# Window attention and two gated MLPs: where the second MLP's weights are decoded

## The chip, the cores and the metric

One NeuronCore of a Trainium2 chip runs the whole program in one launch. The metric is the device time of an execution in microseconds; lower is better. Inputs lie in the chip's DRAM as 64-bit floats, the output is 32-bit. The engines are TensorE (PE, with its weight load PEld), VectorE (DVE), ScalarE (ACT), GpSimd (POOL) and SyncE (SP, which issues the DMAs).

## The reference

Attention over a window of 64 keys (4 x 8 heads, 576 positions, head width 64) gives x of 2304 tokens by 512. Two gated MLPs follow, each with two matrices of 512 by 1536 and one of 1536 by 512:

```python
x = (1 / (1 + np.exp(-(x @ w_gate))) * (x @ w_val)) @ w_out
x = ((x @ w_a) * (x @ w_b)) @ w_out
```

## The kernel before

**Weights.** They come as 64-bit floats, two 32-bit words an element. A weight is *decoded* in bulk: `decode_words` (L369) makes the bits of a 32-bit float from the two words (ScalarE: `low` L374 and `ex` L377; VectorE: `wi` L380, L383 and, for the second MLP, the addition L387), and `decode_pair` (L391) multiplies (L393, VectorE) and splits the weight in a high and a low part (L399 ScalarE, L402 VectorE, GpSimd for `o`), which are multiplied as three products so that the sum is exact enough. F counts the slices of 128 hidden columns: 0 to 11 are the first MLP, 12 to 23 the second (NF = 12). Each F has three matrices, `a`, `b` and `o`. The parts are stored (`save`), to be fetched again for the tokens that come later.

**Tokens.** They are cut into blocks of 256: block 0 alone, 1 to 4 in pairs ("front"), 5 to 8 ("back", a second pass over all weights). For the front's blocks 1 to 4 the second MLP multiplies 2 by 2 blocks with seven products in place of eight. One such set for one F is a *quad* (L912): products 1, 5, 6, 2, 7, 4, 3 in this order, of six matmuls each into three PSUM banks (`qa`, `qb`, `qc`), with sums kept aside in `r` tiles (L865, pool `rs`), sums added (L868), the gate (L878) and the split of the hidden values (L470, L472). Products 5, 6, 7, 3 need sums and differences of the halves of `a` and `b`: `combining` (L416) makes these four *combinations*, each by a GpSimd addition (`s`, L439), a ScalarE copy (`wq`, L441) and a GpSimd subtraction (L442), and stores them.

**Order.** Up to the tenth turn of the first MLP the order on every engine is written out. After that the program gives instructions out in an order of its own, and a scheduler with a timeline simulation makes each engine's queue from it at build: an instruction may go ahead of earlier ones on its engine if the simulation has it ready sooner. An engine runs its queue in order. A manual dependency of class NoSync keeps the scheduler from putting an instruction ahead of another; it makes no wait on the chip.

`step_decode` (L659) does one step of decoding: it finishes one matrix, or one half of a combination. F may be decoded when the buffers of F - 4 are past their last use and F is within `limit`. For the second MLP's quads, `begin_matrix` (L641) starts the words of the next matrix one step ahead of its pair; those of F = NF + 2 are held behind the instruction that stands ahead of the first quad (L1132). The loop at L1139 goes over the twelve quads. In its gaps (`between`, L1160) it takes work off a list (`fill`: the output banks of the two quads before, L984) and takes a decoding step after every product but the fourth. In quad fc, F = NF + fc + 2 is decoded. Ahead of quads 0, 2 and 4, block 0's own hidden values for two F are made (L1141 to L1148: `hidden`, matmuls L461, `hr` L485). The pools of this stretch are opened at L1074. Ahead of the first quad come the last sums of the first MLP (`gacc`, L539; `xh`, `xl`, L570, L571) and the operands of the seven products (L749, L755, L758).

Of the kernel before, what the change touches and what calls it, by code (L numbers as in the profile page):

```python
# [21 lines left out]
def tile_window_attention_gated_mlps(ctx, tc, q, k, v, w1g, w1v, w1o, w2a, w2b, w2o, out):  # L22
# [346 lines left out]
    def decode_words(F, i, nm):  # L369
        st = staged.pop((F, nm))  # L370
        w0, w1 = st[:, :, 0], st[:, :, 1]
        k = 3 * F + i if F > NF + 2 else 0
        low = dec.tile([P, DM], I32, tag="low", name="low")
        nc.scalar.activation(out=low, in_=w0.bitcast(U32), func=AF.Copy, scale=2.0 ** -29)  # L374
        yield
        ex = late["dec"].tile([P, DM], F32, tag="ex", name="ex") if k % 3 == 2 else dec.tile([P, DM], F32, tag="ex", bufs=2, name="ex")
        nc.scalar.activation(out=ex, in_=w1.bitcast(F32), func=AF.Abs)  # L377
        yield
        wi = (late["dec"] if k % 2 else dec).tile([P, DM], I32, tag="wi", name="wi")
        nc.vector.tensor_scalar(  # L380
            out=wi, in0=w1, scalar1=3, scalar2=(1 << 30) - 1, op0=ALU.logical_shift_left, op1=ALU.bitwise_and
        )
        nc.vector.scalar_tensor_tensor(  # L383
            out=wi, in0=w1, scalar=-(1 << 30), in1=wi, op0=ALU.bitwise_and, op1=ALU.bitwise_or
        )
        yield
        (nc.vector if F >= NF else nc.gpsimd).tensor_tensor(out=wi, in0=wi, in1=low, op=ALU.add)  # L387
        wordy[F, nm] = ex, wi
        yield
# [24 lines left out]
    pairs, full = {}, {}  # L414

    def combining(F):  # L416
        got = combinations(parts[F], full.pop((F, "a")), full.pop((F, "b")))
        for half in range(2):
            for n, t in islice(got, 2):
                nc.sync.dma_start(out=kept_q[F - NF][:, n], in_=t.bitcast(F32))  # L420
            yield

    kept_q = [dram.tile([P, 4, 2, CH], F32, tag=f"kq{p}", name=f"kq{p}") for p in range(NF)]

    def halves(got):
        got[1], got[2] = (tuple(p[:, j * CH:(j + 1) * CH] for p in got["a"]) for j in range(2))
        if "b" in got:
            got[4] = tuple(p[:, CH:] for p in got["b"])
# [3 lines left out]
    def combinations(got, a, b):  # L432

        halves(got)
        (a1, a2), (b1, b2) = ((f[:, 0:CH], f[:, CH:]) for f in (a, b))

        def combined(n, nm, x, y, op):
            s = late["sts"].tile([P, CH], F32, tag="s", name=f"s{nm}")
            nc.gpsimd.tensor_tensor(out=s, in0=x, in1=y, op=op)  # L439
            t = late["wq"].tile([P, 2, CH], F32R, tag="wq", name=f"wq{nm}")  # L440
            nc.scalar.activation(out=t[:, 0], in_=s, func=AF.Copy)  # L441
            nc.gpsimd.tensor_tensor(out=t[:, 1], in0=s, in1=t[:, 0].bitcast(F32), op=ALU.subtract)  # L442
            got[nm] = (t[:, 0], t[:, 1])
            return s, (n, t)

        s1, t = combined(0, 5, b1, b2, ALU.add)
        yield t
        s2, t = combined(1, 6, s1, a1, ALU.subtract)
        yield t
        yield combined(2, 7, a1, b1, ALU.subtract)[1]  # L450
        yield combined(3, 3, a2, s2, ALU.subtract)[1]
# [183 lines left out]

    limit = [NF - 1]
    order = [(F, i, nm) for F in range(DECODED, NW) for i, nm in enumerate("abo")]
    held = [None]
    begun, pending, combined_by = [0], [], []

    def begin_matrix():  # L641
        if begun[0] == 0:
            load_weights(DECODED)
        if begun[0] < len(order):
            F, i, nm = m = order[begun[0]]
            begun[0] += 1
            since = len(nc.cur_bb.bb.instructions)
            whole(decode_words(*m))
            if F == NF + 2 and held[0]:
                for i in nc.cur_bb.bb.instructions[since:]:  # L650
                    tc.add_manual_dep(
                        i, held[0],
                        mybir.DependencyInfo(mybir.DependencyClass.NoSync, mybir.DependencyReason.DATA), reason="held",
                    )
            pending.append(m)
            if F + 1 < NW:
                load_matrix(F + 1, nm)

    def step_decode(turn):  # L659

        if combined_by:
            if next(combined_by[0], combined_by) is not combined_by:
                return True
            combined_by.pop()
        if not pending:
            begin_matrix()
        if not pending:
            return False
        F, i, nm = m = pending[0]
        if F > limit[0] or (F > G and last_use.get(F - G - 1, -1) >= turn):  # L670
            return False
        if F >= NF + 2:
            begin_matrix()
        pending.pop(0)
        whole(decode_pair(*m))
        save(F, nm, pairs.pop((F, nm)))
        if nm == "o":
            ready[F] = parts[F]
        elif nm == "b" and F >= NF:
            combined_by.append(combining(F))  # L680
        return True
# [382 lines left out]
    for n, (group, fcs) in enumerate(plan):  # L1064
        begin, end = fcs[0] == 0, fcs[-1] == NF - 1
        if n < len(FIRST):
            continue
        if n == SPAN.start:
            attend(FRONT[-1][-1])
            feed = attention_stream(BACK[BEHIND:])  # L1070
        if n == SPAN.stop:
            attend(BACK[-1])
            attend(steps=100)
            next_part(early, (("op6", 1), ("hs", 1), ("wq", 8), ("sts", 3), ("rs", 2), ("dec", 1)), middle)  # L1074
            limit[0] = NF + 1
        hs = []
        for i, fc in enumerate(fcs):
            need(fc, n)
            hs.append((ready[fc], hidden(0, ready[fc], x[0, group])))
            for _ in range(-(-len(queue) // (len(fcs) - i))):  # L1080
                queue.pop(0)()
            for _ in group:
                for _ in range(2 if late else 1):
                    step_decode(n)
                if late and not combined_by:
                    step_sums()
                if n in SPAN:
                    due += STEPS / ticks
                    attend(steps=int(due))
                    due -= int(due)  # L1090
        queue.append(lambda a=(group_of[group[0]], group, hs, begin, end): [(m(), e()) for m, e in first_projection(*a)])
        if n == len(plan) - 2:
            built = front_operands(FRONT[2], FRONT[1])
            x_ops = next(built)
# [34 lines left out]
    ALONE = {0: (0, 1), 2: (2, 3), 4: (4, 5)}  # L1129
    BETWEEN, LATER = (9, 10, 11), (6, 7, 8)  # L1130
    nquad[0] = 1
    held[0] = next(reversed(nc.cur_bb.bb.instructions)).name  # L1132
    hs, h0s, res = [], [], None
    seconds = (
        lambda: late["hs"].tile([P, 2, W], F32R, tag="hs", name="h1"),
# [3 lines left out]
    for fc in range(NF):  # L1139
# [19 lines left out]

        def between(i):  # L1160
            fill(counts[0][i] + (extra if i == 4 else 0))
            if i != 3:
                step_decode(NEVER)

        hs.append((w["o"], quad(1, w, x_ops, between, g, seconds[fc % 3], lambda: None)))
        if len(hs) == PAIR:
# [161 lines left out]
```

## Time and profile before

| | us |
|---|---|
| median of 3 runs | 962.4 |
| lowest and highest | 962.11, 963.88 |
| the profiled execution | 961.65 |
| its span, first to last instruction | 959.8 |
| granted TensorE clock, mean | 0.996 |

The profile is of one execution. Busy times are of the span or of a stretch of it, in microseconds from its start. A wait is the time in which an engine stood before an instruction, put down to what released it. The rows say `line engine op out<-in`; `st_a` is a staged matrix of words, `wq` a combination, `accm` a bank of the first MLP's output and `accq` one of the second's.

### The profile page before, as it was taken

How to read it: one execution, taken by the hardware profiler on the slowest of the kernel's cores; microseconds unless marked ns; L12 is line 12 of the kernel's file. 1: busy time of each engine (PE TensorE's matmuls, PEld its weight loads, DVE VectorE, ACT ScalarE, POOL GpSimd, SP SyncE). 2: the span in 40 equal slices, each digit the busy share in tenths (PEclk: the TensorE clock that was granted, in tenths of full speed). 3: DMA queues.
4: the chain of work that ended last, by engine and by line, in shares of the span. 5: the costliest groups of instructions: out<-in, count | busy, mean ns of one | idle time of the engine just before them, and what ended most of it. 6: DMA issues, size and time to landing. Idle time of an engine off the chain costs nothing.

```text
span 959.8 us, 15660 instructions
## 1 busy us (share of the span) xinstructions
PE 926.2 (96%) x5504; PEld 774.3 (81%) x5504; DVE 708.0 (74%) x1379; ACT 480.2 (50%) x1063; POOL 311.8 (32%) x321
## 2 busy tenths in 40 slices
PE   7899999999999888899999998999999999999998
PEld 6798888887887777788787886788888888888886
DVE  6997887886568898969989566778888673354545
ACT  7897555687645456654545334654454243211111
POOL 4543222342236727434545127644440000000000
PEclk9999999999999999999999999999999999999999
DMA  8987598988468537755665447354446674554322
GB/s 216 246 240 223 206 327 284 330 287 248 143 229 307 211 142 249 245 202 182 241 217 200 176 155 262 110 176 164 142 155 209 219 263 149 168 167 131 98 66 87
DMA packets 144685, 193.69 MB, mean 202 GB/s; under 512 B 63584, under 2 KB 98912, under 8 KB 143968
## 3 DMA queue, kind: packets, MB, share of 16 engines
q1 hardware_dynamic: 144608, 192.71, 61.9%
q8 instruction: 43, 0.70, 0.3%
q14 instruction: 34, 0.28, 0.1%
HBM read 118.75 MB, written 69.47 MB: 196 GB/s over the span
## 4 chain that ended last, share of the span: by engine, by line
PE 70%; DVE 13%; issue 4%; POOL 4%; DMA 4%; ACT 4%; SPq 0%; DVEq 0%; POOLq 0%; ACTq 0%
PE qa L846 16%; PE accq L984 11%; PE qb L846 8%; PE gps L461 7%; PE vps L461 7%; PE accm L562 6%; PE qc L846 4%; PE accy L947 3%; PE accx L947 2%; POOL s L439 2%; DVE wi L387 2%; DVE wi L383 2%; DVE ex L393 2%; PE xps L228 2%; PE sps L170 1%
## 5 line engine op out<-in xcount | busy, mean ns | idle before, releaser
L865 ACT ACTIVATE r<-qa 128x512 f32<-128x512 f32 x108 | 63.4, 595 | 105.3 <-PE qa L846 95.5
L442 POOL TENSOR_TENSOR wq<-s,wq 128x256 fp32r<-128x256 f32 x96 | 85.4, 895 | 93.0 <-ACT wq L441 88.2
L846 PE MATMUL qa<-op,wq 128*128 128x512 f32 x432 | 112.5, 390 | 0.7 <-ACT op L749 0.6
L846 PE MATMUL qb<-op,wq 128*128 128x512 f32 x432 | 110.5, 390 | 1.5 <-DVE qc L868 1.2
L461 PE MATMUL gps<-xh,wa 128*128 128x256 f32 (+1 forms) x392 | 104.9, 338 | 4.4 <-ACT xh L570 2.3
L461 PE MATMUL vps<-xh,wb 128*128 128x256 f32 (+1 forms) x392 | 105.7, 339 | 3.3 <-ACT hr L485 3.3
L846 PEld LDWEIGHTS qb<-op,wq 128*128 128x128 f32 x432 | 80.9, 188 | 19.0 <-DVE qc L868 1.7
L846 PEld LDWEIGHTS qa<-op,wq 128*128 128x128 f32 x432 | 80.8, 188 | 17.9 <-ACT op L749 0.8
L562 PE MATMUL accm<-hh,wo 128*128 128x512 f32 (+1 forms) x296 | 84.6, 355 | 2.6 <-DVE gacc L539 2.6
L387 POOL TENSOR_TENSOR wi<-wi,low 128x512 int32<-128x512 int32 x36 | 50.0, 1388 | 112.2 <-DVE wi L383 71.3
L461 PEld LDWEIGHTS gps<-xh,wa 128*128 128x128 f32 x392 | 68.7, 189 | 13.8 <-ACT xh L570 2.6
L461 PEld LDWEIGHTS vps<-xh,wb 128*128 128x128 f32 x392 | 69.4, 191 | 11.2 <-ACT hr L485 3.6
L984 PE MATMUL accq<-wo,h 128*128 128x512 f32 (+1 forms) x300 | 71.1, 382 | 1.7 <-DVE resf L988 1.6
L461 PE MATMUL gps<-xl,wa 128*128 128x256 f32 (+1 forms) x196 | 65.8, 336 | 1.0 <-DVE xl L237 0.6
L393 DVE SCALAR_TENSOR_TENSOR ex<-ex,wi 128x512 f32<-128x512 f32 x72 | 52.3, 727 | 18.7 <-ACT ex L377 13.4
L461 PE MATMUL vps<-xl,wb 128*128 128x256 f32 (+1 forms) x196 | 65.9, 336 | 0.0
L984 PEld LDWEIGHTS accq<-wo,h 128*128 128x128 f32 x300 | 55.0, 188 | 13.4 <-DVE resf L988 2.3
L470 ACT ACTIVATE hh<-qa 128x512 fp32r<-128x512 f32 x36 | 21.5, 597 | 84.6 <-DVE qa L878 55.6
L562 PEld LDWEIGHTS accm<-hh,wo 128*128 128x128 f32 x296 | 53.0, 189 | 11.7 <-DVE gacc L539 3.7
L984 PE MATMUL accq<-wo,hh 128*128 128x512 f32 x184 | 55.7, 393 | 3.4 <-ACT hh L470 2.2
L189 ACT ACTIVATE pr<-pr,stat 128x128 f32<-128x128 f32 x144 | 54.0, 390 | 7.5 <-DVE stat L183 7.3
L846 PE MATMUL qa<-op,wa 128*128 128x512 f32 x216 | 57.0, 395 | 0.4 <-DVE g L868 0.4
(178 smaller groups left out, 2137.4 us busy)
## 6 DMA issues: line engine op xcount, KB each, us to landing
wo<-ko SPq DMA_DIRECT2D x27, 512.0 KB, 4.2
wa<-ka SPq DMA_DIRECT2D x27, 512.0 KB, 4.4
st_o<-in_moe_w_out_dram SPq DMA_DIRECT2D x24, 512.0 KB, 4.9
ka<-wa SPq DMA_DIRECT2D x24, 512.0 KB, 4.7
kb<-wb SPq DMA_DIRECT2D x24, 512.0 KB, 3.9
ko<-wo SPq DMA_DIRECT2D x24, 512.0 KB, 4.1
kq<-wq SPq DMA_DIRECT2D x48, 256.0 KB, 3.5
wq<-kq SPq DMA_DIRECT2D x48, 256.0 KB, 3.2
```

The costliest lines, as they stand in the source:

```text
L189: nc.scalar.activation(out=pr[e][:, j, :], in_=pr[e][:, j, :], func=AF.Exp, bias=nmax[:, e, j:j + 1], scale=-1.0, accum_out=None if t in O ...
L228: nc.tensor.matmul(xps[dims, j, rows], lhsT=vv[:, 2 * j + e, :], rhs=pt[e][:, j, rows], start=True, stop=True)
L387: (nc.vector if F >= NF else nc.gpsimd).tensor_tensor(out=wi, in0=wi, in1=low, op=ALU.add)
L393: nc.vector.scalar_tensor_tensor(out=wf, in0=wf, scalar=SMALLEST, in1=wi.bitcast(F32), op0=ALU.is_ge, op1=ALU.mult)
L442: nc.gpsimd.tensor_tensor(out=t[:, 1], in0=s, in1=t[:, 0].bitcast(F32), op=ALU.subtract)
L461: nc.tensor.matmul(ps, lhsT=a[:, c * P:(c + 1) * P], rhs=b[:, c, :], start=(n == 0), stop=(n == 3 * NP - 1))
L470: nc.scalar.activation(out=hh, in_=hr, func=AF.Copy, scale=factor)
L562: nc.tensor.matmul(ps[:, m], lhsT=a[:, sl], rhs=b, start=k == 0, stop=k == total - 1)
L846: nc.tensor.matmul(ps, lhsT=a[:, c * P:(c + 1) * P], rhs=b[:, c, :], start=first and n == 0, stop=n == 5, skip_group_check=True,)
L865: nc.scalar.activation(out=r[n], in_=ps, func=AF.Copy)
L947: nc.tensor.matmul(bank[k], lhsT=a[n][i][:, sl], rhs=b[n][j], start=start and m == 0, stop=m == 2, skip_group_check=True,)
L984: nc.tensor.matmul(ps, lhsT=a, rhs=b, start=n == 0, stop=n == len(pairs) - 1)
```

## The change

The tiles `ex` and `wi` lose their extra buffers, and `begin_matrix` is now called by the step that also finishes the matrix, so no words are made a step ahead; the hold at the first quad goes. A combination is made in three steps: all four sums on GpSimd, then all four copies on ScalarE, then the four subtractions on GpSimd and the stores; the second of them goes together with the next matrix in one call. In the quads the steps are taken by `paced`, which ties the step's instructions, but those of SP, to the last matmul given out ahead of it. Quad 0 takes its six steps two each after products 7, 4 and 3; the others one after every product but the fourth, as before. The pools: `sts` 4 for 3, `rs` 3 for 2, the second `dec` pool gone.

```diff
@@ -369,14 +369,13 @@
     def decode_words(F, i, nm):
         st = staged.pop((F, nm))
         w0, w1 = st[:, :, 0], st[:, :, 1]
-        k = 3 * F + i if F > NF + 2 else 0
         low = dec.tile([P, DM], I32, tag="low", name="low")
         nc.scalar.activation(out=low, in_=w0.bitcast(U32), func=AF.Copy, scale=2.0 ** -29)
         yield
-        ex = late["dec"].tile([P, DM], F32, tag="ex", name="ex") if k % 3 == 2 else dec.tile([P, DM], F32, tag="ex", bufs=2, name="ex")
+        ex = dec.tile([P, DM], F32, tag="ex", bufs=2, name="ex")
         nc.scalar.activation(out=ex, in_=w1.bitcast(F32), func=AF.Abs)
         yield
-        wi = (late["dec"] if k % 2 else dec).tile([P, DM], I32, tag="wi", name="wi")
+        wi = dec.tile([P, DM], I32, tag="wi", name="wi")
         nc.vector.tensor_scalar(
             out=wi, in0=w1, scalar1=3, scalar2=(1 << 30) - 1, op0=ALU.logical_shift_left, op1=ALU.bitwise_and
         )
@@ -414,11 +413,23 @@
     pairs, full = {}, {}
 
     def combining(F):
-        got = combinations(parts[F], full.pop((F, "a")), full.pop((F, "b")))
-        for half in range(2):
-            for n, t in islice(got, 2):
-                nc.sync.dma_start(out=kept_q[F - NF][:, n], in_=t.bitcast(F32))
-            yield
+        got = parts[F]
+        halves(got)
+        (a1, a2), (b1, b2) = ((f[:, 0:CH], f[:, CH:]) for f in (full.pop((F, nm)) for nm in "ab"))
+        sums = {}
+        for nm, x, y, op in ((5, b1, b2, ALU.add), (6, 5, a1, ALU.subtract), (7, a1, b1, ALU.subtract), (3, a2, 6, ALU.subtract)):
+            sums[nm] = s = late["sts"].tile([P, CH], F32, tag="s", name=f"s{nm}")
+            nc.gpsimd.tensor_tensor(out=s, in0=sums[x] if isinstance(x, int) else x, in1=sums[y] if isinstance(y, int) else y, op=op)
+        yield
+        tiles = {}
+        for nm, s in sums.items():
+            tiles[nm] = t = late["wq"].tile([P, 2, CH], F32R, tag="wq", name=f"wq{nm}")
+            nc.scalar.activation(out=t[:, 0], in_=s, func=AF.Copy)
+        yield
+        for n, (nm, t) in enumerate(tiles.items()):
+            nc.gpsimd.tensor_tensor(out=t[:, 1], in0=sums[nm], in1=t[:, 0].bitcast(F32), op=ALU.subtract)
+            got[nm] = (t[:, 0], t[:, 1])
+            nc.sync.dma_start(out=kept_q[F - NF][:, n], in_=t.bitcast(F32))
 
     kept_q = [dram.tile([P, 4, 2, CH], F32, tag=f"kq{p}", name=f"kq{p}") for p in range(NF)]
 
@@ -635,8 +646,8 @@
 
     limit = [NF - 1]
     order = [(F, i, nm) for F in range(DECODED, NW) for i, nm in enumerate("abo")]
-    held = [None]
-    begun, pending, combined_by = [0], [], []
+    parts_done = [0]
+    begun, combined_by = [0], []
 
     def begin_matrix():
         if begun[0] == 0:
@@ -644,34 +655,26 @@
         if begun[0] < len(order):
             F, i, nm = m = order[begun[0]]
             begun[0] += 1
-            since = len(nc.cur_bb.bb.instructions)
             whole(decode_words(*m))
-            if F == NF + 2 and held[0]:
-                for i in nc.cur_bb.bb.instructions[since:]:
-                    tc.add_manual_dep(
-                        i, held[0],
-                        mybir.DependencyInfo(mybir.DependencyClass.NoSync, mybir.DependencyReason.DATA), reason="held",
-                    )
-            pending.append(m)
             if F + 1 < NW:
                 load_matrix(F + 1, nm)
 
     def step_decode(turn):
 
         if combined_by:
-            if next(combined_by[0], combined_by) is not combined_by:
+            parts_done[0] += 1
+            if next(combined_by[0], combined_by) is combined_by:
+                combined_by.pop()
+                parts_done[0] = 0
                 return True
-            combined_by.pop()
-        if not pending:
-            begin_matrix()
-        if not pending:
+            if parts_done[0] == 1:
+                return True
+        if begun[0] == len(order):
             return False
-        F, i, nm = m = pending[0]
+        F, i, nm = m = order[begun[0]]
         if F > limit[0] or (F > G and last_use.get(F - G - 1, -1) >= turn):
             return False
-        if F >= NF + 2:
-            begin_matrix()
-        pending.pop(0)
+        begin_matrix()
         whole(decode_pair(*m))
         save(F, nm, pairs.pop((F, nm)))
         if nm == "o":
@@ -1071,7 +1074,7 @@
         if n == SPAN.stop:
             attend(BACK[-1])
             attend(steps=100)
-            next_part(early, (("op6", 1), ("hs", 1), ("wq", 8), ("sts", 3), ("rs", 2), ("dec", 1)), middle)
+            next_part(early, (("op6", 1), ("hs", 1), ("wq", 8), ("sts", 4), ("rs", 3)), middle)
             limit[0] = NF + 1
         hs = []
         for i, fc in enumerate(fcs):
@@ -1129,7 +1132,19 @@
     ALONE = {0: (0, 1), 2: (2, 3), 4: (4, 5)}
     BETWEEN, LATER = (9, 10, 11), (6, 7, 8)
     nquad[0] = 1
-    held[0] = next(reversed(nc.cur_bb.bb.instructions)).name
+
+    def paced():
+
+        made = nc.cur_bb.bb.instructions
+        since = len(made)
+        at = next(i.name for i in reversed(made) if i.engine == mybir.EngineType.PE)
+        step_decode(NEVER)
+        for i in nc.cur_bb.bb.instructions[since:]:
+            if i.engine != mybir.EngineType.SP:
+                tc.add_manual_dep(
+                    i, at, mybir.DependencyInfo(mybir.DependencyClass.NoSync, mybir.DependencyReason.DATA), reason="paced"
+                )
+
     hs, h0s, res = [], [], None
     seconds = (
         lambda: late["hs"].tile([P, 2, W], F32R, tag="hs", name="h1"),
@@ -1159,8 +1174,8 @@
 
         def between(i):
             fill(counts[0][i] + (extra if i == 4 else 0))
-            if i != 3:
-                step_decode(NEVER)
+            for _ in range(((0, 0, 0, 0, 2, 2, 2) if fc == 0 else (1, 1, 1, 0, 1, 1, 1))[i]):
+                paced()
 
         hs.append((w["o"], quad(1, w, x_ops, between, g, seconds[fc % 3], lambda: None)))
         if len(hs) == PAIR:
```

## Rows read from the trace of the kernel before

**Rows 1.** The page, part 1: busy us, share of the span, instructions.
```profile
PE 926.2 (96%) x5504; PEld 774.3 (81%) x5504; DVE 708.0 (74%) x1379; ACT 480.2 (50%) x1063; POOL 311.8 (32%) x321
```

**Rows 2.** Busy time by stretch; PEclk is the granted clock's mean share.
```profile
core 0: us, PE busy (x) PEld busy (x) DVE busy (x) ACT busy (x) POOL busy (x), PEclk, DMA share, GB/s
...
300.00:336.00 36.00, 32.42 (x150) 26.12 (x149) 31.92 (x47) 16.06 (x32) 23.10 (x21) 1.00 0.67 236
336.00:360.00 24.00, 20.57 (x119) 17.26 (x118) 22.41 (x33) 12.95 (x21) 6.21 (x5) 1.00 0.36 141
360.00:396.00 36.00, 29.58 (x132) 23.75 (x131) 32.85 (x49) 23.08 (x45) 25.33 (x24) 0.95 0.74 251
396.00:532.00 136.00, 132.72 (x625) 110.14 (x624) 119.63 (x185) 75.83 (x147) 62.69 (x66) 1.00 0.61 212
```

**Rows 3.** TensorE's waits, 300 to 532 us: total us, times, longest.
```profile
PE vps L461 <- ACT hr L485: 3.3, 1, 3.3
PE accm L562 <- DVE gacc L539: 2.6, 3, 1.3
PE gps L461 <- ACT xh L570: 2.3, 1, 2.3
PE accq L984 <- ACT hh L470: 2.2, 2, 1.6
...
PE gps L461 <- ACT hr L481: 0.9, 1, 0.9
PE qa L846 <- ACT op L749: 0.6, 1, 0.6
...
PE gps L461 <- DVE xl L571: 0.4, 1, 0.4
```

**Rows 4.** Timeline of GpSimd: start us, us, instruction [idle before <-releaser].
```profile
358.82 4.38 POOL L439 TENSOR_TENSOR s<-ex 128x256 f32<-128x256 f32 x1 [14.75 <-DVE ex L393]
```

**Rows 5.** Timeline of ScalarE, from 314 and from 348 us.
```profile
317.15 0.65 ACT L377 ACTIVATE ex<-st_a 128x512 f32<-128x512 f32 x1
...
348.81 0.67 ACT L374 ACTIVATE low<-st_b 128x512 int32<-128x512 uint32 x1
349.38 0.67 ACT L377 ACTIVATE ex<-st_b 128x512 f32<-128x512 f32 x1
...
363.24 0.42 ACT L441 ACTIVATE wq<-s 128x256 fp32r<-128x256 f32 x1 [3.48 <-POOL s L439]
...
365.60 0.36 ACT L485 ACTIVATE hr<-gps 128x256 f32<-128x256 f32 x1
```

**Rows 6.** Timeline of VectorE, 350 to 367 us.
```profile
351.32 0.42 DVE L380 TENSOR_SCALAR wi<-st_b 128x512 int32<-128x512 int32 x1
...
352.79 0.68 DVE L383 SCALAR_TENSOR_TENSOR wi<-st_b,wi 128x512 int32<-128x512 int32 x1
...
355.73 0.68 DVE L387 CUSTOM_DVE_ANT_0 wi<-wi,low 128x1024 uint16<-128x1024 uint16 x1
...
365.78 0.83 DVE L393 SCALAR_TENSOR_TENSOR ex<-ex,wi 128x512 f32<-128x512 f32 x1 [3.15 <-ACT ex L377]
```

**Rows 7.** VectorE's decoding by line, 316.5 to 326 us: busy us, mean ns.
```profile
L383 DVE SCALAR_TENSOR_TENSOR wi<-st_a,wi 128x512 int32<-128x512 int32 x2 | 1.8, 897 | 0.0
...
L393 DVE SCALAR_TENSOR_TENSOR ex<-ex,wi 128x512 f32<-128x512 f32 x1 | 1.2, 1218 | 0.0
L387 DVE CUSTOM_DVE_ANT_0 wi<-wi,low 128x1024 uint16<-128x1024 uint16 x1 | 1.0, 1012 | 0.1
L380 DVE TENSOR_SCALAR wi<-st_a 128x512 int32<-128x512 int32 x2 | 0.8, 414 | 0.0
```

**Rows 8.** ScalarE's waits, 336 to 532 us: total us, times, longest.
```profile
ACT low L374 <- DVE wi L387: 12.9, 12, 1.8
ACT wq L441 <- POOL s L439: 7.8, 8, 3.5
ACT r L865 <- DVE qc L868: 6.7, 5, 3.0
```

## The prediction

> **What bounds the kernel now.** I read the page's first part, then the busy time by stretch, then TensorE's waits in the stretches with gaps, and last the timelines around the longest wait. TensorE is busy 96% of the span and VectorE 74% [rows 1], so the kernel is bound by TensorE, and what a change can give back is the time in which TensorE stands. By stretch [rows 2] that time is 36 - 32.42 = 3.58 us from 300 to 336 us (end of the first MLP, second MLP's first decoding), 3.43 from 336 to 360 (the operands are made), 6.42 from 360 to 396 (quads 0 to 2) and 3.28 from 396 to 532 (the quads up to the last decoding): 16.7 in all. From 360 to 396 the granted clock is 0.95 on average; if it stood at 1.2 instead of 2.4 GHz for the missing part, that is some 3.6 us at the lower level, 1.8 us of work lost, right behind the longest wait.
>
> In the same stretches VectorE is busy 31.92 of 36, 22.41 of 24, 32.85 of 36 and 119.63 of 136 us [rows 2]: a second limit, close below the first. No wait of TensorE in them is for a DMA [rows 3]. The longest is 3.3 us for ScalarE's `hr` (L485). Its story: GpSimd's first weight sum took 4.38 us [rows 4], ScalarE stood 3.48 us at the copy of that sum (L441), and `hr` was queued behind it [rows 5]; VectorE, out of work, stood 3.15 us for an `ex` in the same queue [rows 6]. So TensorE waited for a decoding step that it did not need until two quads later.
>
> **Part by part.** The work is the same: every F keeps its ScalarE, VectorE and GpSimd instructions and its DMAs. Only places in the queues and five small buffers change, so I price places.
>
> (a) *No words a step ahead, stretch 300 to 336.* The words of F=14 `a` and the first two of F=15 `a` were done here, and F=14's product too. On VectorE they are two L380 (0.8), two L383 (1.8), one L387 (1.0), one L393 (1.2): 4.8 us [rows 7] that move behind quad 0's fifth product. What TensorE gets: before its 0.9 us wait for `hr` (L481) [rows 3] stood an `ex` of F=14 on ScalarE, 0.65 us [rows 5], of which about 0.5 shows. The three waits for `gacc` (2.6 us) have other work ahead of them (F=13's decoding, the sums of the output weights); I leave them. Gain 0.5; bounds 0 and 2.
>
> (b) *Stretch 336 to 360.* ScalarE ran `low` and `ex` of F=14 `b` (0.67 each) just ahead of the operand copies L749 [rows 5], and VectorE ran L380 (0.42), L383 (0.68) and L387 (0.68) between the operand subtractions and the last `gacc` sums [rows 6]. All of it now comes after product 7 of quad 0. The 0.6 us wait for L749 is covered by the 1.3 us of ScalarE; of the 2.3 us wait for `xh` 1.1 (0.42 + 0.68) go; the 0.4 us wait for `xl` is covered by L387 [rows 3]. Sum 2.1; I take 1.9, since the copies may then wait for the first `gacc` sums. Bounds 0 and 3.4.
>
> (c) *Combination in three steps, stretch 360 to 396.* The sums, the copies and the subtractions of an F are now given out a step or more apart, so ScalarE should find the sums done: the 3.3 us wait and the clock's 1.8 behind it are at stake, 5.2 together. But VectorE has little room. Into the stretch come the 4.8 us of (a) and the 1.8 of (b), 6.6; out of it go decoding of F=16 `o` (its four instructions 0.4 + 0.9 + 1.0 + 1.2 = 3.5 by the means of [rows 7]) and the words of F=17 `a` (2.3), because these are now tied to quads 2 and 3: 5.8. Net 0.8 in, against the 3.15 of VectorE's own standing [rows 6] that goes with ScalarE's. VectorE thus allows about 2.4 of the 5.2, and I take 2.4. Bounds 0 and 5.2 for the gain; the loss is the last rival's.
>
> (d) *Stretch 396 to 532.* TensorE's 3.28 us of standing come from VectorE's and ScalarE's evacuations being late; VectorE has 136 - 119.6 = 16.4 us free in it. In this stretch decoding runs until the buffers are full and then stops: ScalarE stood 12.9 us for the one `low` buffer, 7.8 at weight sums and 6.7 at the third `r` of two buffers, each with evacuations queued behind [rows 8]. Steps tied to matmuls, three `r` buffers and no words ahead take most of this away. I take 2.3, 70% of it; bounds 0 and 3.3, with some refilling of the array on top.
>
> (e) *At nothing:* `wi` and `ex` lose a buffer each, since a matrix's words and product are now one chain; the cover is that F is needed two quads after it is decoded. If it goes, the next step's `low` stands on ScalarE as in [rows 8]. The four stores of a combination go out together one step later and stand on SP ahead of later loads and saves; a staged load is used one quad after its issue, so SP has room. In the first MLP up to 300 us the missing words ahead cost nothing as long as a weight is ready before its turn; below nothing is excluded, as TensorE is nearly full there, so 0 to 1 us of loss.
>
> Sum: 0.5 + 1.9 + 2.4 + 2.3 = 7.1. The profiled execution took 961.65 us for a span of 959.8; 961.65 - 7.1 = 954.55. The median of the runs stands 0.75 higher (962.4), so 955.3.
>
> **A rule against it.** GpSimd's 4.38 us sum had its run while VectorE worked without a pause; four sums in a row now stand where VectorE is densest. The Trainium skill ("SBUF — State Buffer", section "Who interferes with whom") says that a VectorE instruction with two SBUF inputs and a GpSimd instruction that reads SBUF exclude each other, the second blocked until the first ends. The row agrees in direction, and by the rule (c) would give nothing in quad 0, the sum then being 4.7. That case is the last rival below.
>
> **Rivals.** *All waits made by decoding go* (chance 0.18). For: most of them stand behind decoding. Against: VectorE would have to be full. Of the 16.7 us and 1.8 of clock the three `gacc` waits of (a) stay, less 2.6 and a little; some 12 to 15 go: 947 to 951.
>
> *VectorE is the limit and takes everything back* (0.13). What is gained before 360 us is paid in quads 0 to 2, where F=14 and F=15 are decoded together before block 0's own pass over them. For: 91% busy there already. Against: its 3.15 us of standing. 0.5 + 1.9 are gained and as much lost: 962.4, within 2 either way.
>
> *Slower: quad 0's bunch* (0.15). In quad 0 the steps are given out two at a time, and the sums of F=14 and their copies are tied to the same matmul, product 4's or a bank's behind it. If GpSimd is held as in [rows 4], ScalarE stands at the copies again, so the 3.3 and 1.8 us stay; VectorE's 6.6 us of added work then falls into the stretch with its 3.15 us of standing not recovered, and F=15 `b` is late for the pass of block 0: 6.6 less the 2.4 gained before, 4.2 lost, 966.6. It decides at the copies: if the first sum ends later than ScalarE reaches its copy by more than about a microsecond.
>
> **How the numbers follow.** The forecast of 7.1 us has the chance 0.54, with its own range from 951 to 960.4. The range for 8 in 10 takes in the first rival down to 947 and the slower side up to 965. A difference of 0.2% (1.9 us) is about what a measurement of this kernel can tell. Faster: 0.54 + 0.18 = 0.72; same 0.13; slower 0.15.
>
> **What would show it.** (a) No `low` or L380 of F=14 before quad 0; the first after 355 us. (b) The waits for L749, `xh` and `xl` shrink to below 1.5 together. (c) No wait of `vps` for L485 over 1 us, and L441's wait for L439 below 2 us in the quads; granted clock 1.00 from 360 to 396. (d) `low`'s wait for L387 below 4 us. VectorE's busy time stays about the same, its share rises. Wrong if TensorE stands over 6 us between 360 and 396, above all in the pass of block 0 over F=14 and F=15 waiting for decoding, or if gaps appear before 300 us.

## The result and the profile after

| us | before | after |
|---|---|---|
| median of 4 runs each | 963.14 | 953.71 |
| lowest and highest | 962.11, 967.04 | 951.43, 955.45 |
| the profiled execution | 961.65 | 955.45 |
| its span | 959.8 | 953.5 |
| its granted clock, mean | 0.996 | 0.998 |

The ratio is 0.9907, interval 0.9889 to 0.9924: the change takes 9.4 us off, 7.3 to 10.7 by the interval; 7.1 was forecast. The profiled execution of after is its slowest; the two runs whose granted clock is 1.000 on average took 951.43 and 952.30, so one drop of the clock more or less is part of the scatter.

After's page, part 1: the engines do the same work, in less time [rows 1].

```profile
PE 925.9 (97%) x5504; PEld 773.1 (81%) x5504; DVE 708.4 (74%) x1379; ACT 478.8 (50%) x1063; POOL 303.3 (32%) x321
```

After, busy time by stretch (us of the span; PE, PEld, DVE, ACT, POOL, then clock and DMA), to be read against [rows 2]:

```profile
300.00:336.00 36.00, 34.51 (x157) 27.17 (x156) 29.14 (x43) 16.18 (x32) 21.52 (x23) 1.00 0.71 265
336.00:360.00 24.00, 23.09 (x135) 19.66 (x135) 22.27 (x33) 14.14 (x25) 2.91 (x4) 1.00 0.21 83
360.00:396.00 36.00, 33.58 (x162) 27.98 (x161) 32.38 (x50) 21.64 (x45) 19.56 (x18) 0.95 0.74 258
396.00:532.00 136.00, 133.77 (x616) 110.53 (x615) 124.59 (x194) 76.80 (x148) 63.62 (x66) 1.00 0.63 214
```

TensorE stands 1.49, 0.91, 2.42 and 2.23 us in the four stretches, 7.05 in all, where it stood 16.7. VectorE's share from 396 to 532 us rises from 119.6 to 124.6 of 136. After, TensorE's waits from 300 to 532 us (total, times, longest):

```profile
PE qa L849 <- ACT r L868: 2.9, 3, 1.9
...
PE accm L573 <- DVE gacc L550: 1.3, 3, 0.6
...
PE qa L849 <- ACT op L752: 0.3, 1, 0.3
```

The waits for `hr`, `xh` and `xl` of [rows 3] are gone; the longest left is 1.9 us for an `r`.

**Where the time came from.** To place the gain I took, from each trace, the time at which as many matmul columns had been given out as before's trace had at a given time, and subtracted. From the same work at 291 us on (until then the order is written out or untouched; the executions differ by -0.6 to +3.1 us there, from the first 60 us on), the differences to before are, in us:

| kernel | 342 | 367 | 403 | 483 | 532 | 563 | 616 |
|---|---|---|---|---|---|---|---|
| after | -1.0 | -7.9 | -8.7 | -10.0 | -10.8 | -9.3 | -8.0 |
| untied | +1.8 | +3.5 | -1.9 | -4.3 | -5.4 | -3.2 | -3.1 |
| before, tied | -1.0 | -7.4 | -10.2 | -8.7 | -6.8 | -5.0 | -5.0 |
| two `r` buffers | -1.8 | -8.5 | -10.7 | -8.7 | -9.1 | -8.6 | -8.4 |
| quad 0 even | -1.7 | -5.4 | -8.7 | -10.0 | -10.7 | -9.3 | -8.5 |
| halves | -1.7 | -8.6 | -12.2 | -14.6 | -12.1 | -4.0 | -4.0 |
| halves, late `o` | -1.4 | -8.2 | -12.7 | -13.7 | -16.1 | -6.8 | -6.8 |
| the same, in order | -1.7 | -8.6 | -13.0 | -14.0 | -16.5 | -12.6 | -8.7 |
| six steps, `o` fifth | -1.4 | -8.2 | -11.8 | -14.2 | -10.8 | -1.2 | -0.3 |
| six steps, `o` last | -1.8 | -8.7 | -13.2 | -14.7 | -16.9 | -15.1 | -14.6 |

(Times are before's. One execution each, so a difference of one or two microseconds between two rows says little. The kernels are those of the next section.) After gains 1.0 up to 342 us, 6.9 more up to 367, where before had its wait for `hr`, 2.9 more up to 532, and gives 2.8 back behind 532 us, where the quads end and the last blocks' operands are loaded (called the border below). A stretch of lower clock counts in its row: half of the full clock was granted for 3.4 us from 366.7 in before, for 3.4 from 387.6 in after and for 6.8 from 362.6 in untied, each by its own time.

### The profile page after: what moved, and what is told of

It reads as the page before. It is cut to its first block, busy times and chain, and to the rows that moved or that the text cites. A ratio compares the mean times of both kernels' runs of the same rounds, so it can differ in the third digit from the quotient of the medians.

```text
span 953.5 us, 15652 instructions
## 1 busy us (share of the span) xinstructions
PE 925.9 (97%) x5504; PEld 773.1 (81%) x5504; DVE 708.4 (74%) x1379; ACT 478.8 (50%) x1063; POOL 303.3 (32%) x321
## 4 chain that ended last, share of the span: by engine, by line
PE 69%; DVE 14%; DMA 5%; POOL 4%; ACT 4%; issue 3%; SPq 0%; DVEq 0%; POOLq 0%; ACTq 0%
PE qa L849 16%; PE accq L987 11%; PE qb L849 8%; PE gps L472 7%; PE vps L472 6%; PE accm L573 6%; PE qc L849 4%; PE accy L950 3%; PE accx L950 2%; DVE ex L392 2%; DVE wi L382 2%; PE xps L228 2%; DVE wi L379 1%; DVE wi L386 1%; DMA st_o<-in_moe_w_out_dram 1%
## 5 line engine op out<-in xcount | busy, mean ns | idle before, releaser
L392 DVE SCALAR_TENSOR_TENSOR ex<-ex,wi 128x512 f32<-128x512 f32 x72 | 53.3, 741 | 14.6 <-ACT ex L376 7.4
L849 PE MATMUL qa<-op,wb 128*128 128x512 f32 x216 | 55.2, 391 | 1.9 <-ACT r L868 1.9
L849 PE MATMUL qc<-op,wa 128*128 128x512 f32 x216 | 56.9, 390 | 0.0
```

What stands on the lines that cost most here:

```text
L392: nc.vector.scalar_tensor_tensor(out=wf, in0=wf, scalar=SMALLEST, in1=wi.bitcast(F32), op0=ALU.is_ge, op1=ALU.mult)
L849: nc.tensor.matmul(ps, lhsT=a[:, c * P:(c + 1) * P], rhs=b[:, c, :], start=first and n == 0, stop=n == 5, skip_group_check=True,)
```

## The experiments

**Theory:** the gain comes from the place of the decoding, that is from the tie. **Rivals:** it comes from the combination in three steps; or from the third `r` buffer; and bunching quad 0's steps matters or does not. The first four runs take one part each back out.

**Untied.** The steps are given out as before, by the scheduler's choice.

```diff
-                paced()
+                step_decode(NEVER)
```

> The changed kernel, its steps in the same places of the program but not tied to the last matmul; nothing else. Theory A (the place of decoding is what counts): the scheduler puts decoding ahead again, VectorE decodes F=14 before quad 0, and 4 to 6 of the 9.4 us come back: 957.5 to 960. Theory B (the three-step combination and the free ScalarE queue are what counts): at most 2 come back: 953.7 to 956.

Measured: 958.67 us (10 runs), ratio 0.9962 [0.9949, 0.9975]: 5.0 of after's 9.4 us go, as theory A had it. Its stretches:

```profile
300.00:336.00 36.00, 32.60 (x139) 24.95 (x138) 33.80 (x50) 18.26 (x35) 23.06 (x21) 1.00 0.79 278
336.00:360.00 24.00, 19.66 (x115) 16.68 (x113) 23.63 (x33) 13.37 (x25) 12.77 (x12) 1.00 0.50 183
```

Its longest waits of TensorE from 300 to 400 us:

```profile
PE accm L573 <- DVE gacc L550: 4.0, 6, 1.0
PE gps L472 <- ACT xh L581: 4.0, 1, 4.0
```

Its timeline of VectorE (start, us), the first word instruction of F=14 `a` and `o`:

```profile
319.50 0.41 DVE L379 TENSOR_SCALAR wi<-st_a 128x512 int32<-128x512 int32 x1
...
332.87 0.43 DVE L379 TENSOR_SCALAR wi<-st_o 128x512 int32<-128x512 int32 x1
```

Without the tie the scheduler puts the words of all of F=14 ahead of the first quad, and VectorE is late with the operands that TensorE needs there: the table reads +3.5 at 367 us, 11 us behind after, of which the 6.8 us at half the clock, from the end of the 4.0 us wait on, are 3.4. Of the 11, 6.5 come back by 616: F=14 is then done already, and after has a late `r` and lower clock of its own behind 384 us. In after the first of these instructions stands at 355.87, in VectorE's timeline, where the tie wants it:

```profile
355.87 0.42 DVE L379 TENSOR_SCALAR wi<-st_a 128x512 int32<-128x512 int32 x1
```

**Halves.** After, but the combinations as before: two halves of two, each sum, copy and subtraction in a row, and the step accounting that goes with it (`o` comes in the fifth of a quad's six slots, after product 4).

```diff
     def combining(F):
...
+        got = combinations(parts[F], full.pop((F, "a")), full.pop((F, "b")))
+        for half in range(2):
+            for n, t in islice(got, 2):
+                nc.sync.dma_start(out=kept_q[F - NF][:, n], in_=t.bitcast(F32))
+            yield
...
         if combined_by:
+            if next(combined_by[0], combined_by) is not combined_by:
                 return True
+            combined_by.pop()
```

> The changed kernel with the combination made as before, two of the four at a time, each sum, copy and subtraction in a row; tied, no words ahead, three r buffers. Theory B: ScalarE stands at a copy for 3 us again in quad 0 and 3 to 5 us come back: 957 to 959. Theory A: under 1.5 come back: 953.7 to 955.2.

Measured: 960.55 us (10 runs), ratio 0.9975 [0.9963, 0.9986], but not as either side had it: in the quads up to 483 us the halves are ahead of after (-14.6 against -10.0 in the table), and the 3.3 us wait for `hr` does not come back. All is lost behind 483 us, in two places. First, ScalarE's timeline from 490 us (start, us, instruction, idle before and its releaser):

```profile
490.59 0.67 ACT L373 ACTIVATE low<-st_b 128x512 int32<-128x512 uint32 x1 [2.22 <-DVE wi L386]
491.72 0.67 ACT L376 ACTIVATE ex<-st_b 128x512 f32<-128x512 f32 x1 [0.46 <-POOL wo L401]
492.29 0.58 ACT L469 ACTIVATE hh<-qa 128x512 fp32r<-128x512 f32 x1
```

and TensorE's:

```profile
492.93 1.20 PE L971 MATMUL accq<-wo,hh 128*128 128x512 f32 x4 [2.48 <-ACT hh L469]
```

An `hh` that TensorE needs at once stands behind the words of `b`, which wait for the addition of the matrix before. Second, the border. SP's timeline (its durations are those of the issue with what it waits for):

```profile
537.13 0.79 SPq L1177 DMA_DIRECT2D xq<-bx  x2
...
538.64 4.57 SPq L419 DMA_DIRECT2D kq<-wq  x4
543.30 0.91 SPq L1177 DMA_DIRECT2D xq<-bx  x2
```

ScalarE's:

```profile
550.75 1.06 ACT L781 ACTIVATE op<-xq 128x1024 fp32r<-128x1024 f32 x1 [5.03 <-DMA xq<-bx]
551.71 0.58 ACT L852 ACTIVATE r<-qa 128x512 f32<-128x512 f32 x1
```

TensorE's:

```profile
552.34 2.17 PE L833 MATMUL qa<-op,wb 128*128 128x512 f32 x5 [4.81 <-ACT r L852]
```

and GpSimd's:

```profile
539.77 3.10 POOL L441 TENSOR_TENSOR wq<-s,wq 128x256 fp32r<-128x256 f32 x3
```

SP stands 4.57 us at the four stores of a combination, whose last three subtractions GpSimd ends only at 542.87; behind them stands the second pair of operand loads; ScalarE waits 5.03 us for these at the operand copy `op`, and behind `op` stands the `r` for which TensorE waits 4.81. The granted clock then falls to 0.5, the lower level, for 3.4 us. Three queues in order, one chain. In before SP's timeline has the four loads together:

```profile
538.84 2.61 SPq L1178 DMA_DIRECT2D xq<-bx  x4
```

**Two `r` buffers.**

```diff
-            next_part(early, (("op6", 1), ("hs", 1), ("wq", 8), ("sts", 4), ("rs", 3)), middle)
+            next_part(early, (("op6", 1), ("hs", 1), ("wq", 8), ("sts", 4), ("rs", 2)), middle)
```

> The changed kernel with two r buffers in place of three. If ScalarE's standing at the third r (6.7 us before) held up evacuations that TensorE waited for: 2 to 4 us come back, 955.7 to 957.7. If it stood there with nothing urgent behind it, as the forecast's sum has it (no term for it): 953.7 to 954.7.

Measured: 953.64 us (4 runs), ratio 0.9904 [0.9882, 0.9926]: level with after: no gain of the third buffer is resolved. By the table its trace is 2.0 us ahead of after at 403 us, as it has no lower clock there, and then loses 1.6 up to 532, where after gains 2.1; so within the quads the third buffer may be worth something that these runs do not show in the time.

**Quad 0 even.** Its steps one by one like those of the other quads.

```diff
-            for _ in range(((0, 0, 0, 0, 2, 2, 2) if fc == 0 else (1, 1, 1, 0, 1, 1, 1))[i]):
+            for _ in range((1, 1, 1, 0, 1, 1, 1)[i]):
```

> The changed kernel with quad 0's steps one after every product but the fourth, as in the other quads, in place of two each after the last three; tied. By the forecast's term (b) the words of F=14 then stand again between the operands: about 2 us come back, 955 to 956.5. If quad 0's bunch costs what it saves (the slower rival's mechanism, only smaller): 952 to 954.

Measured: 954.6 us (4 runs), ratio 0.9916 [0.989, 0.9942], not resolved from after. The profile shows the cost where the forecast's step (b) put it (2.5 us less gained at 367 us). By 403 us the two are level, since after has lost 1.9 us to its late `r` and 1.7 to the lower clock by then, and this execution has no wait for an `r` over 1 us there and a clock of 1.000.

**Tied alone.** The kernel before with `paced` and quad 0's slots, without the other parts; the hold ahead of the first quad goes with it, since the tie takes its place. Words a step ahead, halves, and two `r` buffers stay.

```diff
-            if i != 3:
-                step_decode(NEVER)
+            for _ in range(((0, 0, 0, 0, 2, 2, 2) if fc == 0 else (1, 1, 1, 0, 1, 1, 1))[i]):
+                paced()
```

> The kernel before with one thing of the change: its steps tied to the last matmul and quad 0's taken two by two; words still a step ahead in their extra buffers, combination in halves, two r buffers. Theory A: the tie alone holds F=14's later words back, but F=14 a, begun before, stays in the first MLP: 3 to 6 us faster than before, 956.5 to 959.5. If the ties help only together with the words not being ahead: 960 to 963.

Measured: 957.71 us (5 runs), ratio 0.9951 [0.9933, 0.9969], 4.6 below the median of before measured with it (962.35). Up to 403 us it has all of after's gain (-10.2 against -8.7), then it loses 5.2 us up to 616, 3.4 of them in the quads, where after gains. So the tie gives the gain ahead of and in the first quads; the rest of the change is needed to keep it. Which part of the rest keeps it is not shown: the halves, which have the tie and no words ahead, keep it up to 483 us without the three steps, but no run takes out the words ahead alone.

**The border.** Is it the scheduler's order on ScalarE that loses at the border what the halves had gained? From the last quad to the border every kernel here holds VectorE to the order in which the program gives its instructions out; these two hold ScalarE too, one made from after, one from the halves.

```diff
-    in_order(eased, (mybir.EngineType.DVE,))
+    in_order(eased, (mybir.EngineType.DVE, mybir.EngineType.Activation))
```

> The changed kernel with ScalarE's order, like VectorE's already, kept as written from quad 11 to the block 0 passes behind it, so that the next phase's operand copies can't stand ahead of quad 11's r and h. If part of the gain is given back at that border (2.0 us from 532 to 547 us and 1.3 from 555 to 600 in the profile of the change): 951 to 953. If the border costs nothing by its order: 953.7, or later by a wait of the pass for the copies.

> The same border order put on the kernel with the combination in halves (960.6 without it). Theory C (the three-step combination gains nothing within the quads; the halves lost at the border alone, where ScalarE stood 5 us for the next phase's load ahead of quad 11's r): 951.5 to 954.5, within 1.5 of the run with three steps and this order. Theory B (the three steps themselves gain): 957 to 960.

Measured: 954.69 us (4 runs) for after with it, 959.4 (5 runs) for the halves: 0.9916 [0.9896, 0.9935] and 0.9961 [0.994, 0.9982]. No gain for after, and the 1.2 us of the halves is within the two intervals. In the halves' trace the order does remove the 4.8 us wait for `r` (from 532 to 563 us 3.4 are lost in place of 8.1, from -10.9 to -7.5), though the stores still stand 4.56 us; but 2.3 more go up to 616. ScalarE's order alone doesn't give back what the halves had gained.

**Six steps, `o` last.** The step that copies no longer takes `o` with it, so an F takes six steps: `a`, `b`, sums, copies, subtractions, `o`; `o` comes after product 3.

```diff
-            if parts_done[0] == 1:
-                return True
+            return True
```

> The changed kernel with the copies and the next matrix in steps of their own (six steps for an F: a, b, sums, copies, subtractions, o). ScalarE's 1.9 us late r at 386 us stood behind four copies, an ex, a low and an ex given out together; if that bunch costs, the wait and the lower clock behind it go: 951 to 953. If o a step later makes F late: 954 to 957.

Measured: **947.06 us** (4 runs), ratio 0.9839 [0.9822, 0.9857]: 6.6 us faster than after, 4 below the range expected, and the best of all that computes the whole. Its stretches:

```profile
360.00:396.00 36.00, 35.35 (x184) 30.10 (x183) 34.16 (x54) 22.71 (x46) 19.45 (x18) 1.00 0.73 250
396.00:532.00 136.00, 135.49 (x617) 111.86 (x616) 126.78 (x196) 77.94 (x149) 67.94 (x68) 1.00 0.65 223
```

SP's timeline at the border:

```profile
532.17 2.91 SPq L432 DMA_DIRECT2D kq<-wq  x4
...
536.73 0.83 SPq L1192 DMA_DIRECT2D xq<-bx  x2
```

and ScalarE's:

```profile
542.43 1.06 ACT L796 ACTIVATE op<-xq 128x1024 fp32r<-128x1024 f32 x1 [3.01 <-PE qa L848]
```

TensorE is busy 35.35 of 36 and 135.49 of 136 us in the quads. The stores stand ahead of the second pair of loads here too, but for 2.91 us, and the pair goes out 5.7 us ahead of its `op`, which waits for TensorE's matmuls into `qa` and no longer for the load.

**Three steps or the place of `o`?** Three runs part the two, and a fourth asks what VectorE still costs.

Halves with `o` in the last slot:

```diff
-            for _ in range(((0, 0, 0, 0, 2, 2, 2) if fc == 0 else (1, 1, 1, 0, 1, 1, 1))[i]):
+            for _ in range(((0, 0, 0, 0, 2, 2, 2) if fc == 0 else (1, 1, 1, 0, 1, 0, 1))[i]):
```

> The combination in halves as in the run of that name (960.6), with the matrix o taken after product 3, the last, in place of product 4. Theory D (what counts in the later quads is how evenly the steps stand, o not next to the copies): 953 to 956.5. Theory B (the order sum, copy, subtraction in a row is what costs): 958.5 to 961.5.

Measured: 955.97 us (4 runs), ratio 0.9927 [0.9912, 0.9942], 4.6 below the halves. Up to 532 us it is level with six steps and `o` last (-16.1 and -16.9); the 9.3 us between 532 and 563 are the border's chain again, with the stores held 4.56 us.

Six steps with `o` fifth, after product 4, ahead of the subtractions:

```diff
-            parts_done[0] += 1
-            if next(combined_by[0], combined_by) is combined_by:
-                combined_by.pop()
-                parts_done[0] = 0
-                return True
-            if parts_done[0] == 1:
+            if parts_done[0] < 2 or order[begun[0] % len(order)][2] != "o" or begun[0] == len(order):
+                parts_done[0] += 1
+                if next(combined_by[0], combined_by) is combined_by:
+                    combined_by.pop()
+                    parts_done[0] = 0
                 return True
```

> The changed kernel with six steps for an F as in the run with all steps alone (947.1), but o ahead of the subtractions: a, b, sums, copies, o, subtractions. If it is enough that copies and o are not given out together: 946.5 to 949. If o has to come last (the subtractions early, so the quad two later and the stores on SP have them): 950 to 954.

Measured: 962.27 us (10 runs), ratio 1.0 [0.9984, 1.0016]: the whole gain is gone, beyond both ranges: 15 us from two neighbouring steps that change places. TensorE's longest waits from 480 to 620 us:

```profile
PE qa L848 <- ACT r L867: 8.3, 4, 4.9
PE accq L986 <- ACT hh L481: 3.0, 1, 3.0
```

SP's timeline at the border:

```profile
541.74 4.57 SPq L432 DMA_DIRECT2D kq<-wq  x4
546.40 0.91 SPq L1192 DMA_DIRECT2D xq<-bx  x2
```

and ScalarE's:

```profile
553.93 1.06 ACT L796 ACTIVATE op<-xq 128x1024 fp32r<-128x1024 f32 x1 [5.09 <-DMA xq<-bx]
```

These are the halves' two places, in a kernel with three steps: the late `hh` and the stores held 4.57 us ahead of the loads. So neither needs the halves. The late `hh` goes with the place of `o`: with `o` late the halves' longest wait for an `hh` is 0.7 us. The held stores do not go with it alone, since they stand 4.56 us in the halves with `o` late too; only with six steps and `o` last are they held less.

Halves, late `o`, and ScalarE's order held at the border:

> The combination in halves, o after product 3, and ScalarE's order kept at the border from quad 11 on. Theory D and E together (within the quads the three steps gain nothing; in the run without the border order 9 us went between 531 and 563 us, where ScalarE stood 5 us for the next phase's load ahead of quad 11's last r): 947 to 950.5, near the run with all steps alone (947.1). If the halves cost by themselves at the end (the stores holding SP, the copies holding ScalarE): 952.5 to 956.

Measured: 952.84 us (4 runs), ratio 0.9894 [0.9877, 0.991], 3.1 below the kernel without the order, 5.8 above six steps with `o` last. With the order held, up to 563 us 3.8 are lost instead of 9.3, but 4 more follow between 581 and 599, with a clock of 0.5 for 6.8 us. The stores still stand 4.58 us, but no `op` stands ahead of the `r` now, and the 4.89 us wait for that `r` is gone: with these two runs the last link of the chain is shown. The 4 us further on have the same form: ScalarE stands 3.51 us at 581.21 for an `op` whose input VectorE makes late, an `r` is queued behind it, TensorE waits 1.96 us for that `r` until 583.10, and the lower clock takes 3.4 more.

Is VectorE the limit? Six steps, `o` last, without one VectorE instruction of each matrix from F = 14 on:

```diff
-        (nc.vector if F >= NF else nc.gpsimd).tensor_tensor(out=wi, in0=wi, in1=low, op=ALU.add)
+        if F < NF + 2:
+            (nc.vector if F >= NF else nc.gpsimd).tensor_tensor(out=wi, in0=wi, in1=low, op=ALU.add)
```

> The run with all steps alone (947.1), without the addition of the low word's bits for F = 14 and on: 30 VectorE instructions of some 0.9 us, 27 us in all, are left out, and with them the last three bits of these weights. If VectorE is what still bounds the stretch and the border behind it (3.8 us of waits for output sums): 942 to 945. If TensorE is the only limit left in the quads: 945.5 to 947.5.

Measured: 943.89 us (2 runs only), ratio 0.9802 [0.9782, 0.9823], in the first of the two ranges; the interval just touches that of the kernel with the instruction. The stretches:

```profile
360.00:396.00 36.00, 36.00 (x185) 30.84 (x184) 27.82 (x46) 24.70 (x50) 16.97 (x18) 1.00 0.70 245
396.00:532.00 136.00, 135.97 (x622) 113.06 (x621) 113.88 (x176) 75.54 (x147) 65.12 (x72) 1.00 0.69 240
```

VectorE is busy 19 us less in these two stretches (34.16 + 126.78 against 27.82 + 113.88) and the kernel gains 3.2 (947.06 - 943.89): TensorE had 1.2 us left to gain in them; and from 532 to 616 us this kernel loses 1.1 (from -18.3 to -17.2), the one with the instruction 2.3.

## Why the prediction was right, and where its steps were not

The time (955.3 against 953.71), its sign and its main reason held: decoding off the path of the first quads. That the time came so near is in part luck: by the table (c) gave 2.8 us more than its term, and 2.8 came back behind 532 us, where the sum had no term. Step by step, by the table:

**(a) Held in direction, size within its bounds.** Forecast 0.5, bounds 0 to 2; 1.0 gained up to 342 us. No word of F=14 stands before 355 us, and the wait of `accm` for `gacc`, which I had left alone, fell from 2.6 to 1.3 us: less of VectorE's work stands ahead of the sums (29.14 us busy from 300 to 336, where it was 31.92).

**(b) Right.** Forecast 1.9; TensorE's standing from 336 to 360 us fell from 3.43 to 0.91, by 2.5. The waits for `op`, `xh` and `xl`, 3.3 in [rows 3], are 0.3. The even quad 0 shows that the late slots matter at this place: 2.5 us at 367.

**(c) The wait went, but its size and its reason were wrong.** I put 5.2 us at stake, of which VectorE would allow 2.4. From 342 to 384 us after gains 8.2 (-1.0 to -9.2); less the 2.5 of (b) this is 5.7, all of the 5.2 that the wait and the clock behind it had cost, and 0.5 is lost from there to 403. The mis-sized term is VectorE's ceiling of 2.4: it took the 3.15 us of VectorE's own standing in [rows 6], less 0.8 of added work, for all the room there was. After's VectorE is busy 32.38 us in this stretch, no more than before's 32.85. With six steps and `o` last VectorE was busy 34.16 of these 36 us while TensorE was busy 35.35. And the reason given, sums a step ahead of their copies, is not what removes the wait: the halves with the tie have no such wait (-8.6 at 367), and before with the tie alone has none over 0.7 us from 340 to 380 (-7.4). What these have in common is the place of the whole chain, behind the operands' VectorE work. What would show it, the wait of the copy L427 for the sum L422, came out against me: in total it stays, only the longest shrinks [rows 8]. After, ScalarE's waits from 336 to 532 us:

```profile
ACT low L373 <- DVE wi L386: 18.2, 13, 2.8
...
ACT wq L427 <- POOL s L422: 7.5, 18, 0.9
```

The mean clock from 360 to 396 stayed at 0.95 too, for a new reason: four copies stood one after the other for sums given out only a step earlier, `ex` of `o` between them and the words of the next `a` behind, and then an `r`. After's timeline of ScalarE:

```profile
382.02 0.42 ACT L427 ACTIVATE wq<-s 128x256 fp32r<-128x256 f32 x1 [0.64 <-POOL s L422]
383.17 0.42 ACT L427 ACTIVATE wq<-s 128x256 fp32r<-128x256 f32 x1 [0.72 <-POOL s L422]
383.49 0.66 ACT L376 ACTIVATE ex<-st_o 128x512 f32<-128x512 f32 x1
384.32 0.42 ACT L427 ACTIVATE wq<-s 128x256 fp32r<-128x256 f32 x1 [0.17 <-POOL s L422]
384.64 0.65 ACT L373 ACTIVATE low<-st_a 128x512 int32<-128x512 uint32 x1
385.20 0.65 ACT L376 ACTIVATE ex<-st_a 128x512 f32<-128x512 f32 x1
385.76 0.57 ACT L868 ACTIVATE r<-qa 128x512 f32<-128x512 f32 x1
```

and of TensorE:

```profile
386.39 1.96 PE L849 MATMUL qa<-op,wq 128*128 128x512 f32 x6 [1.89 <-ACT r L868]
```

Behind this wait the granted clock fell to 0.5 for 3.4 us. With six steps, where the copies and `o` are apart, no wait for an `r` from 300 to 620 us is longer than 1.0.

**(d) Right in size, by other reasons.** Forecast 2.3; 2.1 gained between 403 and 532 us. But ScalarE's standing for `low` grew, from 12.9 to 18.2, where I had asked for less than 4, and the `r` buffer, whose 6.7 us of standing I counted on (after has no wait of `r` for VectorE in this stretch), gives no gain that the time resolves. The total of such standing is no price: after stands longer for `low` than before and is faster. What the stretch is seen to depend on is how the steps lie: from 403 to 532 six steps with `o` last gain 3.7, with `o` fifth they lose 1.0.

**(e) Not at nothing, but by other waits than the stores'.** I said that the four stores of a combination, going out together, have room on SP since a load is used one quad after its issue. At the border they do stand ahead of operand loads. After's SP timeline there:

```profile
530.63 1.37 SPq L1193 DMA_DIRECT2D xq<-bx  x2
...
533.65 2.67 SPq L432 DMA_DIRECT2D kq<-wq  x2
536.41 0.38 SPq L1193 DMA_DIRECT2D xq<-bx  x1
```

and ScalarE's, after and then before:

```profile
544.38 1.06 ACT L797 ACTIVATE op<-xq 128x1024 fp32r<-128x1024 f32 x1 [3.54 <-DMA xq<-bx]
```

```profile
547.59 1.06 ACT L794 ACTIVATE op<-xq 128x1024 fp32r<-128x1024 f32 x1 [3.38 <-DMA xq<-bx]
```

In after no wait of TensorE's comes of it: `op` stood as long for its load in before, and TensorE, which has output sums to multiply meanwhile, has no wait from 534 to 562 us of after's profile. In the halves and with `o` fifth, `op` stands 5.0 and 5.1 us with an `r` queued behind it, and those lose 8.1 and 9.6 us from 532 to 563, where after loses 1.5. The 2.8 us that after gives back lie elsewhere. TensorE's waits from 532 to 620 us, before:

```profile
PE accq L984 <- DVE resf L988: 1.6, 2, 1.3
PE acc L514 <- DVE resf L988: 1.5, 1, 1.5
```

and after:

```profile
PE accq L987 <- DVE resf L991: 3.7, 2, 2.5
...
PE qb L849 <- POOL wq L430: 0.6, 1, 0.6
```

The 1.5 us up to 563 hold two waits of 0.6: this one for a combination's subtraction on GpSimd, and at 528.27 one for an `hh`. The 1.3 us behind 563 are mostly VectorE's sums of the output (`resf`), for which TensorE waits 4.1 us in all (0.4 of it in `acc`) where before waited 3.1. The forecast ended at 532 us and had no term for either. Nothing was lost ahead of 300 us beyond the first 60 us, which differ from run to run.

**The rivals.** *All waits go* (947 to 951): the change as made doesn't reach it, one line more does (947.06). *VectorE takes everything back*: false; VectorE at 126.78 of 136 us leaves TensorE 135.49, and 19 us less of VectorE's work in the quads bring 3.2. *Quad 0's bunch*: false at its place: the first sum was not held. After's timeline of GpSimd, the first and the longest of the four sums of F=14:

```profile
365.51 0.98 POOL L422 TENSOR_TENSOR s<-ex 128x256 f32<-128x256 f32 x1 [23.96 <-DVE ex L392]
...
367.60 1.24 POOL L422 TENSOR_TENSOR s<-ex 128x256 f32<-128x256 f32 x1
```

The longest took 1.24 us, not 4.38 [rows 4], though VectorE ran without a pause here too. The difference in the traces is what it ran: in before, four of the five instructions that start within the long sum read two tiles of SBUF, the last of them ends at 362.6 us and the sum at 363.2; in after, evacuations that read PSUM stand between (`hl` L483 twice, `g` L871, `qc` L881). That agrees with the rule of the Trainium skill ("SBUF — State Buffer", section "Who interferes with whom"), by which a VectorE instruction with two SBUF inputs contends with a GpSimd instruction that reads SBUF. If so, GpSimd got through between those instructions in after; no run here varies this mix alone.

**What stays open:** why the halves, with `o` late and ScalarE's order held, are still 5.8 us behind the six steps. Their loss lies behind 532 us (7.8 us up to 616, against 2.3), 4.2 of it between 581 and 599 us by the wait and the lower clock told above; why `op` and `r` stand in this order in that kernel and not with six steps was not tested.

## What to carry to other kernels

Where a scheduler fills queues that run in order, tie background work to the foreground work that it must not overtake, then spread it one small step per gap: two steps at one tie cost 6.6 us here, and two neighbouring steps in the wrong order 15. Count a queue's standing time as a loss only after naming what stands behind it; 6.7 us of it on ScalarE for an `r` buffer left no mark in the time, and the kernel with 18.2 for `low` is faster than the one with 12.9, while 4.57 us at stores on SP ended, through three queues, in a wait of 4.8 on TensorE in the halves, and 2.67 in after in none. And look at the place where the pattern of a loop ends: a store that has room inside the loop may stand ahead of a load of what comes next.

## What was not expected of the hardware

The granted clock fell to 0.5 for 3.4 us behind a TensorE wait of 1.9 us in after's profile and for 3.4 behind one of 4.8 us in the halves', so that there a late evacuation cost more than its wait. It did not fall in the quads of six steps with `o` last, nor behind a wait of 2.0 us for an `r` in the profile with two `r` buffers or of 2.5 us for an `hh` in the halves': the length of the wait alone does not tell. The written-out first 60 us, which no edit here is meant to touch, differed by up to 3.7 us from one profiled execution to another (-0.6 with two `r` buffers, +3.1 untied), over a third of the whole gain: a single profile against a single profile would have misjudged this change.
